# A retention and expert kernel: the first expert in plain fp32, zeroed columns in the activations, one program order on every engine

## The chip, the cores and the metric

The kernel runs on one core of a Trainium2 chip. The metric is the device time of one execution in microseconds (us). The core has five engines with queues of their own, each of which works strictly in the order of its instructions: PE (TensorE, the matmuls; "PEld" is its loading of weights), DVE (VectorE), ACT (ScalarE), POOL (GpSimd) and SP (SyncE, which here only issues DMA transfers). POOL issues the indirect transfers, those that scatter rows to addresses held in a table. Engines wait for one another by semaphores.

## What is computed

Two stages follow each other. The first is a retention layer (attention with a decay and no softmax) over 8 batches, 8 heads, 576 positions and head size 64; its output is read as 4608 tokens of 512 numbers. The second is a mixture of experts: 16 experts in 4 groups of 4. Each token goes to one expert, chosen by two argmaxes, and is scaled by the product of the two softmax weights.

```python
scores = scale * np.matmul(q, k.transpose(0, 1, 3, 2))
ret = scores * Dmat[None, :, :, :]            # Dmat = gamma ** (i - j) for i >= j, else 0
x = np.matmul(ret, v)                         # -> (4608, 512)
...
for g in range(G):                            # 4 groups
    ...
    for e in range(Eg):                       # 4 experts in each
        mask_e = e_idx == e
        h = np.maximum(xg[mask_e] @ w1[g, e], 0.0)      # 512 -> 1024
        ye = h @ w2[g, e]                               # 1024 -> 512
        combined = g_w[mask_g][mask_e] * e_w[mask_e]
        out[tok_idx] = combined[:, None] * ye
```

All inputs and the output are fp32, and an expert's weights are 4 MB.

## The kernel before

**Attention.** The 36 token tiles of 128 (`t`) go through a software pipeline, the loop at line 618: `scale(t + 1)` makes the decayed values `vs` (eight small ACT copies a tile; for the last four tiles one POOL operation), `scores(t)` (PE, then the mask on DVE, `sT`), `av(t - 1)`, `state(t)` and `inter(t - 1)` (PE; DVE writes the tile's x transposed, `xT`), and behind them by some tiles `logits`, `gate`, `places` (which expert a token goes to and its place in that expert's list) and `xnat`, which turns x, scales it and scatters its rows with an indirect transfer to the DRAM table `xs`, sorted by expert. Attention's matmuls are plain fp32.

**The order of experts.** The passes `p` = 0 to 15 run over the experts by load: the two fullest are picked early (`pick(0)` and `pick(1)`), the others are ranked by count once all tokens are placed (`rank_experts`, a run of DVE operations). Each pass has a fixed capacity of columns, `CAPS`, from 356 for p = 1 down to 260 for p = 15. Pass 0 takes the first 256 tokens of the fullest expert, and the last pass, p = 16, the rest of that expert's 384. What doesn't fit is left to a loop at the end.

**One expert.** `xload` (SP) fetches the expert's rows of x in 32-row blocks (`xb`), `xturn` transposes them on DVE into `xTf`, `xsplit` splits them in two fp32r parts, high (ACT copy, `xTh`) and low (DVE subtraction, `xTl`). Each weight piece (four for each expert, w1 and w2) is loaded raw (`r`), and `split` makes its high and low parts, `wh` on ACT and `wl` on DVE, two halves each. A product is then three fp32r matmuls: high by high, high by low, low by high. `layer1(p, f)` makes 128 of the 1024 hidden units: 12 matmuls into `ph`, ACT's relu `hh` (high part) and DVE's `hl` (low part). `layer2(p, f)` adds them to the sums `py` in PSUM with another 12 matmuls (p = 0 and 16 lay tokens on the output rows instead, and p = 0 takes 6). Eight values of f make an expert. PE runs `layer1(p, f)` and then `layer2` of the step before, so that the last layer2 of an expert comes behind the first layer1 of the next. There `yturn` (DVE) transposes the four finished sums out of PSUM, and `ystore` scatters them to `out` with POOL's indirect transfers, two blocks of 32 tokens in each of the following steps.

DVE transposes in blocks of 32, so where a capacity is no multiple of 32, the columns of `py` up to the next multiple must hold numbers. `layer2` zeroes them by a memset of each of the four sums at f = 0, ahead of its matmuls:

```python
            if not natural(p) and CS[p] % 32:
                for py in pys[p]:
                    dve.memset(py[:, CS[p] : 32 * nblocks(p)], 0.0)
```

`xpad(p)` is one more indirect POOL transfer: it zeroes the 128 rows behind an expert's tokens in `xs`, ahead of that expert's `xload`. The code issues one in each pass, two passes ahead.

**Queues and their order.** Every engine call goes through the wrapper `Ordered` (line 95), whose one line, 106, is therefore the line of nearly every instruction in the profile; instructions are told apart by their tiles. `pin` (line 91) ties an instruction behind the one that stands before it in its engine's list, by `keep_in_program_order`. Instructions that the wrapper doesn't see, such as the register moves in front of an indirect transfer, are not tied themselves, and a transfer pinned behind such a move is free to go where the move goes. Within these ties a scheduler chooses the order when the kernel is built.

Of the kernel before, what the change touches and what calls it, by code (L numbers as in the profile page):

```python
# [15 lines left out]
P = 128  # L16
# [4 lines left out]
E = G * EG  # L21
# [44 lines left out]
def moe_retention(ctx, tc, qk, kv, wgt, w1, w2, c_f, out):  # L66
# [23 lines left out]

    def pin(inst):
        tc.keep_in_program_order(inst)
        return inst
# [59 lines left out]
    def split_piece(i, part):  # L153
        if i < len(pieces):
            wsp[i, part] = wsplit(*pieces[i], raws[i], part)

# [80 lines left out]
    def xturn(p, part, of):  # L237

        if part == 0:
            xTs[p] = xpair(f"m{p}")  # L240
            xTf[p] = ring(f"xTf_{p}")[:, 0 : NKC * CMAX].rearrange("p (k c) -> p k c", k=NKC)
        nb = nblocks(p)
        b0, b1 = nb * part // of, nb * (part + 1) // of
        dve.transpose(
            xTf[p][:, :, 32 * b0 : 32 * b1].rearrange("p k (b t) -> p b k t", t=32),
            xg[p][:, b0:b1, 0:DQ].rearrange("p b (k f) -> p b k f", f=32),
        )
# [172 lines left out]
    def pick(j):  # L420


        def t_(nm, n=1):
            return sm.tile([P, n], F32, name=f"{nm}{j}", tag=nm)

        eh = eah[j]
        pc = ps_sm.tile([P, E], F32, name=f"pc{j}", tag="sm")
        pe.matmul(pc, ones, ohc, start=True, stop=True)
        k0 = t_("k0", E)
        dve.scalar_tensor_tensor(k0, pc, float(E), eid, ALU.mult, ALU.subtract)  # L430
        if j:
# [9 lines left out]
        picked[j] = f0  # L441
        if j:
            return

        k2 = t_("k2", E)
        dve.tensor_tensor(k2, eh, pc, ALU.mult)
        c0 = t_("c0")
# [12 lines left out]
    with ExitStack() as ac:  # L460
# [58 lines left out]
        def scale(t):  # L519

            T = tiles[t]
            T["vs"] = ap.tile([P, H, D], F32, name=f"vs_{t}", tag="vs", bufs=3)
            if t >= PICK + 6:

                pool.tensor_tensor(
                    T["vs"], T["v"], gk[:, T["c"], :].unsqueeze(2).to_broadcast([P, H, D]), ALU.mult
                )
                return
# [89 lines left out]
        for t in range(NT + 1):  # L618
# [26 lines left out]
            if r == 5:  # L645
                pick(0)
                expert_of(0)
            if r in (5, 6, 7, 9):
                load_piece((5, 6, 7, 9).index(r))
            if r == 7:  # L650
                xload(0)
                split(0)
            if r == 8:
                split(1)
                for i in range(2):
                    xturn(0, i, 2)
            if t == NT:
                for kc in range(NKC):
                    xsplit(0, kc)
                split(2)  # L660
# [6 lines left out]
    def count_experts():  # L667
# [7 lines left out]
        pad(pad1, picked[1], n1, 32 * nblocks(1))  # L675
        xpad(1)

    def rank_experts():
# [18 lines left out]
        with nc.allow_low_precision("integers below 16"):  # L697
            dve.tensor_reduce(order, kk, AX.X, ALU.add)

# [7 lines left out]
        dve.tensor_scalar(mia, kk[:, :, 0:NB], float(BIG), None, ALU.mult)  # L707
        cb, ce = [sm.tile([P, E], F32, name=f"c{x_}", bufs=1) for x_ in "be"]
# [10 lines left out]
    def layer1(p, f):  # L719
        i = p * NPIECE + f // 2  # L720
        C = CS[p]
        wh, wl = wsp[i, 0]
        xh, xl = xTs[p]
# [5 lines left out]
        cs = slice((f % 2) * P, (f % 2) * P + P)  # L729
        n = 0  # L730
# [6 lines left out]
        hh = mp.tile([P, CMAX], F32R, name=f"hh_{p}_{f}", tag="hh", bufs=4)  # L737
# [7 lines left out]
    def layer2(p, f):  # L745
        if f == 0:
# [4 lines left out]
            if not natural(p) and CS[p] % 32:  # L751
                for py in pys[p]:
                    dve.memset(py[:, CS[p] : 32 * nblocks(p)], 0.0)
        C = CS[p]
        wh, wl = wsp[p * NPIECE + f // 2, 1]
        hh, hl = hts.pop((p, f))
        st_, sp_ = f == 0, f == NFC - 1
        if natural(p):
            for i, (r0, n) in enumerate(ttiles(p)):
                py = pys[p][i]  # L760
                for m, (a, b) in enumerate(((hh, wh), (hh, wl), (hl, wh))):
                    pe.matmul(
                        py[:n], a[:, r0 : r0 + n], b[:, f % 2, :], start=st_ and m == 0, stop=sp_ and m == 2
                    )
            return
        for dc in range(NKC):
            py = pys[p][dc]
            ds_ = slice(dc * P, (dc + 1) * P)
            pe.matmul(py[:, :C], wh[:, f % 2, ds_], hh[:, :C], start=st_, stop=False)
# [70 lines left out]
    prev = None  # L840
    for p in range(E):
        for f in range(NFC):
# [17 lines left out]
            split(2 * pc + f % 2 + 3)  # L860
# [14 lines left out]
            if (p, f) == (0, 4):  # L875
                rank_experts()
# [3 lines left out]
            if f == (2 if p > 0 else 5) and p + 2 <= E:  # L880
# [308 lines left out]
```

## Time and profile before

| | us |
|---|---|
| median of three runs | 733.26 |
| lowest and highest | 727.58, 739.38 |
| the profiled execution | 735.81 |
| its span, first to last instruction | 734.0 |
| attention, to the first matmul of p = 0 | 173.7 |
| p = 0, to the first matmul of p = 1 | 31.9 |
| p = 1 to 15, to the first matmul of the last pass | 498.9 |
| the last pass and the end | 29.6 |

The profile is of one execution. Its page gives busy time by engine, groups of instructions and the chain of waits; other views cut the span in stretches, list the instructions in order of time, or sum up who waited for whom. A row such as "PE py <- DVE py: 48.1, 14, 13.8" says that PE's instructions that write `py` waited for a DVE instruction that writes `py`: 48.1 us in all, 14 times, at most 13.8. In a row of a timeline stand start, duration, engine, operation, output and inputs, shapes, how many, and in brackets the idle time ahead of it and what ended it. "PEclk" is the TensorE clock that was granted, as a share of full speed. The releaser "remote" stands for a semaphore whose sender the profile couldn't place in time.

### The profile page before, as it was taken

The numbers are of one execution on the slowest core, as the hardware profiler recorded it, in microseconds if no ns is written. First come the engines' busy times: TensorE is split into PE (matmuls) and PEld (weight loads), VectorE is DVE, ScalarE is ACT, GpSimd is POOL, SyncE is SP. The second block draws the span as 40 slices with busy tenths as digits, with TensorE's granted clock in tenths as the row PEclk, the third lists the DMA queues.
The fourth block names the chain that finished last, engine by engine and source line by source line (L and its number), as shares of the span: only waits on it lengthen the run. The fifth ranks groups of instructions, "written<-read, shape, count | busy, mean of one in ns | idle before, by whom it ended". The sixth has DMA issues, their size and how long they took to land.

```text
span 734.0 us, 15587 instructions
## 1 busy us (share of the span) xinstructions
PE 633.8 (86%) x5707; PEld 589.3 (80%) x5707; DVE 447.8 (61%) x1093; ACT 325.7 (44%) x829; POOL 230.4 (31%) x258
## 2 busy tenths in 40 slices
PE   7999999987847979878979889898998988889891
PEld 6778787766737979878969889898898988889891
DVE  2677777779843639584637384655656638366580
ACT  3877677534432424332515253343434525335360
POOL 0032222342470060835050505224152140422532
PEclk8999999999987999998999899999999999999997
DMA  9998898573887653149555474646567567465200
GB/s 341 408 387 305 297 332 283 206 254 128 268 257 239 195 167 116 36 137 314 152 152 153 148 207 143 200 134 177 168 194 219 157 179 204 136 184 152 92 16 22
DMA packets 63262, 144.22 MB, mean 196 GB/s; under 512 B 9393, under 2 KB 30393, under 8 KB 63184
## 3 DMA queue, kind: packets, MB, share of 16 engines
q1 hardware_dynamic: 52640, 121.00, 52.5%
q0 software_dynamic: 9248, 20.35, 7.6%
q10 hardware_dynamic: 1296, 1.86, 0.7%
q8 instruction: 46, 0.75, 0.4%
q14 instruction: 32, 0.26, 0.1%
HBM read 122.84 MB, written 24.88 MB: 201 GB/s over the span
## 4 chain that ended last, share of the span: by engine, by line
PE 46%; issue 13%; DVE 6%; POOL 5%; ACT 2%; another core or an unknown queue 2%; DMA 1%; POOLq 0%; ACTq 0%
PE py L106 23%; PE ph L106 22%; DVE wl L106 3%; POOL out L106 3%; ACT wh L106 1%; DVE y L106 1%; POOL xs L106 1%; ACT hh L106 1%; PE phn L106 1%; DMA xs<-zero,pads 1%; DVE hl L106 0%; PE pxt L106 0%; POOL ov_big L106 0%; POOL ov_small L106 0%
## 5 line engine op out<-in xcount | busy, mean ns | idle before, releaser
L106 POOL DMA_INDIRECT out<-y,ii x152 | 156.9, 1032 | 335.1 <-DVE y L106 293.3
L106 PE MATMUL py<-hh,wh 128*128 128x356 f32 (+14 forms) x480 | 151.8, 316 | 59.2 <-DVE py L106 48.1
L106 ACT ACTIVATE hh<-ph 128x256 fp32r<-128x256 f32 (+15 forms) x128 | 53.9, 421 | 298.3 <-PE ph L106 208.6
L106 DVE SCALAR_TENSOR_TENSOR hl<-ph,hh 128x256 fp32r<-128x256 f32 (+15 forms) x128 | 59.3, 464 | 198.7 <-ACT hh L106 156.7
L106 DVE TENSOR_TENSOR wl<-r,wh 128x512 fp32r<-128x512 f32 x272 | 176.8, 692 | 5.2 <-ACT wh L106 1.7
L106 PE MATMUL ph<-xTh_m,wh 128*128 128x256 f32 (+15 forms) x512 | 160.1, 313 | 1.8 <-ACT xTh_m L106 1.2
L106 PE MATMUL ph<-xTl_m,wh 128*128 128x256 f32 (+15 forms) x512 | 159.3, 311 | 0.9 <-issue 0.6
L106 PE MATMUL ph<-xTh_m,wl 128*128 128x256 f32 (+15 forms) x512 | 158.5, 310 | 0.4 <-issue 0.4
L106 PE MATMUL py<-hl,wh 128*128 128x356 f32 (+14 forms) x480 | 151.8, 316 | 4.0 <-DVE hl L106 4.0
L106 ACT CAST wh<-r 128x512 fp32r<-128x512 f32 x272 | 153.7, 617 | 0.0
L106 PE MATMUL py<-hh,wl 128*128 128x356 f32 (+14 forms) x480 | 149.9, 312 | 0.0
L106 PEld LDWEIGHTS py<-hh,wh 128*128 128x128 f32 x480 | 94.7, 197 | 64.5 <-issue 34.4
L106 PEld LDWEIGHTS ph<-xTh_m,wh 128*128 128x128 f32 x512 | 102.8, 201 | 2.1 <-ACT xTh_m L106 1.4
L106 PEld LDWEIGHTS ph<-xTl_m,wh 128*128 128x128 f32 x512 | 102.2, 200 | 2.3 <-issue 1.7
L106 PEld LDWEIGHTS ph<-xTh_m,wl 128*128 128x128 f32 x512 | 101.6, 198 | 1.2 <-issue 1.1
L106 PEld LDWEIGHTS py<-hl,wh 128*128 128x128 f32 x480 | 95.3, 199 | 6.8 <-DVE hl L106 6.8
L106 PEld LDWEIGHTS py<-hh,wl 128*128 128x128 f32 x480 | 95.0, 198 | 0.0
L106 POOL DMA_INDIRECT xs<-xt,sl x36 | 37.0, 1028 | 141.2 <-ACT vs L106 41.4
L106 ACT ACTIVATE vs<-b,cf 128x64 f32<-128x64 f32 x256 | 64.4, 336 | 4.8 <-DMA b<-in_kv 4.8
L106 DVE TENSOR_TENSOR sT<-pss,masks 128x512 f32<-128x512 f32 x72 | 46.2, 683 | 28.0 <-PE pss L106 26.5
L106 PEld LDWEIGHTS pss<-a 64*128 64x128 f32 x576 | 39.4, 192 | 18.4 <-DVE sT L106 8.8
L106 PE MATMUL pss<-a 64*128 64x128 f32 x576 | 48.5, 293 | 5.2 <-DVE sT L106 2.9
(160 smaller groups left out, 604.3 us busy)
## 6 DMA issues: line engine op xcount, KB each, us to landing
r<-in_w SPq DMA_DIRECT2D x138, 512.0 KB
a<-in_qk SPq DMA_DIRECT2D x35, 512.0 KB
b<-in_kv SPq DMA_DIRECT2D x35, 512.0 KB
xb<-xs SPq DMA_DIRECT2D x24, 148.5 KB
xb<-xs SPq DMA_DIRECT2D x20, 165.0 KB
out<-y,ii POOLq DMA_INDIRECT x152
xb<-xs SPq DMA_DIRECT2D x12, 181.5 KB
gq<-c_f ACTq DMA_DIRECT2D x5, 256.0 KB
```

Source lines behind the costliest of these rows:

```text
L106: i_ = f(*a, **k)
```

## The change

- **First expert whole.** For p = 0 (`whole(p)`) the weights and x aren't split. `layer1` is four plain fp32 matmuls, raw w1 by `xTf`, `layer2` one for each of the two token tiles, and the relu writes fp32; `hl`, `xsplit(0)` and the splits of the first eight half pieces are gone.
- **Zeroed columns.** The memsets of `py` are gone. `layer1` at f = 0 zeroes the columns of `hh` from the capacity to the next multiple of 32, and the first matmul of each sum at f = 0 runs over these columns too.
- **Program order.** `pin` now ties each wrapped instruction to the last wrapped instruction of the same engine, whatever stands between.
- **Ranking in parts.** `rank_experts` is a generator: the order of experts at (0, 4), the tables for unused places at (0, 5), the rest at (0, 6), where the register for p = 2 is loaded too. `xpad(2)` moves from (0, 5) to (0, 7), and `xturn(1)` and `xsplit(1)` one step later.
- **Around the first expert.** `pick(0)` is cut in two: its second half, `close`, runs one tile later. `xload(0)` comes one tile earlier, the two halves of `xturn(0)` stand in two tiles instead of one, and `scale` uses ACT for all tiles.

```diff
     def pin(inst):
-        tc.keep_in_program_order(inst)
+
+        i_ = inst.ins
+        if i_.engine in last:
+            tc.add_manual_dep(
+                i_, last[i_.engine].name,
+                mybir.DependencyInfo(mybir.DependencyClass.NoSync, mybir.DependencyReason.DATA),
+                reason="order of the program",
+            )
+        last[i_.engine] = i_
         return inst
...
-            xTs[p] = xpair(f"m{p}")
+            xTs[p] = None if whole(p) else xpair(f"m{p}")
...
-            if t >= PICK + 6:
-
-                pool.tensor_tensor(
-                    T["vs"], T["v"], gk[:, T["c"], :].unsqueeze(2).to_broadcast([P, H, D]), ALU.mult
-                )
-                return
...
+            if r == 6:
+                close()
             if r in (5, 6, 7, 9):
                 load_piece((5, 6, 7, 9).index(r))
-            if r == 7:
+            if r == 6:
                 xload(0)
-                split(0)
-            if r == 8:
-                split(1)
-                for i in range(2):
-                    xturn(0, i, 2)
+            if r in (8, 9):
+                xturn(0, r - 8, 2)
             if t == NT:
-                for kc in range(NKC):
-                    xsplit(0, kc)
-                split(2)
                 ids(0)
...
+        hh = mp.tile([P, CMAX], F32R, name=f"hh_{p}_{f}", tag="hh", bufs=4)
+        if whole(p):
+            for kc in range(NKC):
+                pe.matmul(
+                    ph[:, :C], raws[i][0][:, kc, cs], xTf[p][:, kc, :C], start=kc == 0, stop=kc == NKC - 1
+                )
+            act.activation(hh[:, :C].bitcast(F32), ph[:, :C], AF.Relu)
+            hts[p, f] = (hh.bitcast(F32), None)
+            return
...
+        C32 = 32 * nblocks(p)
+        if f == 0 and C32 > C:
+
+            dve.memset(hh[:, C:C32].bitcast(F32), 0.0)
...
-            if not natural(p) and CS[p] % 32:
-                for py in pys[p]:
-                    dve.memset(py[:, CS[p] : 32 * nblocks(p)], 0.0)
...
-                for m, (a, b) in enumerate(((hh, wh), (hh, wl), (hl, wh))):
+                ab = ((hh, wh),) if whole(p) else ((hh, wh), (hh, wl), (hl, wh))
+                for m, (a, b) in enumerate(ab):
...
+        C0 = 32 * nblocks(p) if st_ else C
...
-            pe.matmul(py[:, :C], wh[:, f % 2, ds_], hh[:, :C], start=st_, stop=False)
+            pe.matmul(py[:, :C0], wh[:, f % 2, ds_], hh[:, :C0], start=st_, stop=False)
...
-            split(2 * pc + f % 2 + 3)
+            if 2 * pc + f % 2 + 3 >= 2 * NPIECE:
+                split(2 * pc + f % 2 + 3)
...
-            if (p, f) == (0, 4):
-                rank_experts()
+            if (p, f) in ((0, 4), (0, 5)):
+                next(ranks, None)
+            if (p, f) == (0, 6):
+                next(ranks, None)
+                expert_of(2)
...
-            if f == (2 if p > 0 else 5) and p + 2 <= E:
+            if f == (2 if p > 0 else 7) and p + 2 <= E:
                 xpad(p + 2)
...
-            if f == NFC - 3:
+            if f == (NFC - 3 if p else NFC - 2):
                 for i in range(3):
                     xturn(p + 1, i, 3)
-            if f == NFC - 2:
+            if f == (NFC - 2 if p else NFC - 1):
                 for kc in range(NKC):
                     xsplit(p + 1, kc)
```

More of the change, by code (lines that the diff above doesn't have):

```diff
@@ L89, in moe_retention @@
     ones = cp.tile([P, P], BF16, name="ones")
+    last = {}
     def pin(inst):
-        tc.keep_in_program_order(inst)
+        i_ = inst.ins
[6 more added lines that the diff above has]
+        last[i_.engine] = i_
         return inst
@@ L155, in split_piece, with whole @@
             wsp[i, part] = wsplit(*pieces[i], raws[i], part)
+    def whole(p):
+        return p == 0
     def split(k):
@@ L440, in pick, with close @@
         dve.tensor_copy(eai[j], f0)
-        picked[j] = f0
-        if j:
-            return
-        k2 = t_("k2", E)
+        picked[j] = f0, pc
+    def close():
+        f0, pc = picked[0]
+        eh = eah[0]
+        k2 = sm.tile([P, E], F32, name="k2")
         dve.tensor_tensor(k2, eh, pc, ALU.mult)
-        c0 = t_("c0")
+        c0 = sm.tile([P, 1], F32, name="c0")
         dve.tensor_reduce(c0, k2, AX.X, ALU.add)
@@ L522, in scale @@
             T["vs"] = ap.tile([P, H, D], F32, name=f"vs_{t}", tag="vs", bufs=3)
-            if t >= PICK + 6:
-                pool.tensor_tensor(
-                    T["vs"], T["v"], gk[:, T["c"], :].unsqueeze(2).to_broadcast([P, H, D]), ALU.mult
-                )
-                return
             for h in range(H):
@@ L674, in count_experts @@
         dve.tensor_reduce(n1, c1, AX.X, ALU.add)
-        pad(pad1, picked[1], n1, 32 * nblocks(1))
+        pad(pad1, picked[1][0], n1, 32 * nblocks(1))
         xpad(1)
@@ L698, in rank_experts @@
             dve.tensor_reduce(order, kk, AX.X, ALU.add)
+        yield
         cr = sm.tile([P, E], F32, name="cr")
@@ L707, in rank_experts @@
         dve.tensor_scalar(mia, kk[:, :, 0:NB], float(BIG), None, ALU.mult)
+        yield
         cb, ce = [sm.tile([P, E], F32, name=f"c{x_}", bufs=1) for x_ in "be"]
@@ L721, in layer1 @@
         C = CS[p]
-        wh, wl = wsp[i, 0]
-        xh, xl = xTs[p]
         if p == 0:
@@ L729, in layer1 @@
         cs = slice((f % 2) * P, (f % 2) * P + P)
+        hh = mp.tile([P, CMAX], F32R, name=f"hh_{p}_{f}", tag="hh", bufs=4)
[7 more added lines that the diff above has]
+            return
+        wh, wl = wsp[i, 0]
+        xh, xl = xTs[p]
         n = 0
@@ L736, in layer1 @@
                 n += 1
-        hh = mp.tile([P, CMAX], F32R, name=f"hh_{p}_{f}", tag="hh", bufs=4)
+        C32 = 32 * nblocks(p)
+        if f == 0 and C32 > C:
+            dve.memset(hh[:, C:C32].bitcast(F32), 0.0)
         hl = mp.tile([P, CMAX], F32R, name=f"hl_{p}_{f}", tag="hl", bufs=4)
@@ L750, in layer2 @@
             ]
-            if not natural(p) and CS[p] % 32:
-                for py in pys[p]:
-                    dve.memset(py[:, CS[p] : 32 * nblocks(p)], 0.0)
         C = CS[p]
-        wh, wl = wsp[p * NPIECE + f // 2, 1]
+        wh, wl = (raws[f // 2][1], None) if whole(p) else wsp[p * NPIECE + f // 2, 1]
         hh, hl = hts.pop((p, f))
@@ L760, in layer2 @@
                 py = pys[p][i]
-                for m, (a, b) in enumerate(((hh, wh), (hh, wl), (hl, wh))):
+                ab = ((hh, wh),) if whole(p) else ((hh, wh), (hh, wl), (hl, wh))
+                for m, (a, b) in enumerate(ab):
                     pe.matmul(
-                        py[:n], a[:, r0 : r0 + n], b[:, f % 2, :], start=st_ and m == 0, stop=sp_ and m == 2
+                        py[:n], a[:, r0 : r0 + n], b[:, f % 2, :],
+                        start=st_ and m == 0, stop=sp_ and m == len(ab) - 1,
                     )
             return
+        C0 = 32 * nblocks(p) if st_ else C
         for dc in range(NKC):
@@ L840, in moe_retention @@
     prev = None
+    ranks = rank_experts()
     for p in range(E):
```

## The prediction

> **What bounds the kernel now.** I began with the page, to see which engine could set the end.
>
> ```profile
> span 734.0 us, 15587 instructions
> PE 633.8 (86%) x5707; PEld 589.3 (80%) x5707; DVE 447.8 (61%) x1093; ACT 325.7 (44%) x829; POOL 230.4 (31%) x258
> ```
>
> PE is the busiest, yet 14% of the span has no matmul in it. An average over stages says nothing about where. So the second view was busy time by stretch, cut at the first layer-1 matmul of each expert (columns: stretch, its length, then busy time of PE, PEld, DVE, ACT, POOL, the granted clock, the DMA share, GB/s). First all fifteen experts of 24 matmul groups each (p = 1 to 15) in one row, then four of them (p = 1, 2, 9 and 10).
>
> ```profile
> 205.53:704.42 498.89, 433.80 (x2875) 424.11 (x2874) 291.03 (x621) 195.39 (x426) 164.34 (x157) 0.94 0.57 168
> ```
>
> ```profile
> 205.53:252.94 47.41, 33.35 (x187) 32.50 (x186) 20.85 (x44) 16.24 (x34) 12.00 (x12) 0.86 0.76 235
> 252.94:287.78 34.84, 30.84 (x194) 30.05 (x193) 19.98 (x44) 13.35 (x28) 12.80 (x13) 1.00 0.54 162
> ...
> 497.29:529.64 32.35, 28.13 (x195) 27.48 (x193) 18.46 (x41) 12.73 (x29) 10.24 (x10) 0.95 0.59 169
> 529.64:555.81 26.17, 26.17 (x195) 25.73 (x193) 16.38 (x33) 11.96 (x28) 10.65 (x10) 1.00 0.67 193
> ```
>
> The row at 529.64 is the find of this profile. It is p = 10, whose capacity is 288. It takes 26.17 us, has PE busy for all of it and the clock at 1.00. Its neighbour in the row above (292 columns, 1.4% more work) takes 32.35 us. 288 is the only capacity from 356 down to 260 that is a multiple of 32, so it is the one expert for which layer2 issues no memset of its sums. The third view, the waits, says the same thing:
>
> ```profile
> PE py L106 <- DVE py L106: 48.1, 14, 13.8
> PE py L106 <- ACT hh L106: 11.0, 8, 3.6
> PE py L106 <- DVE hl L106: 4.0, 2, 2.2
> DVE ov_bt L106 <- POOL ov_small L106: 5.8, 1, 5.8
> ```
>
> PE waited 14 times, once for each of the other fourteen, for "DVE py", which is that memset: 48.1 us, one time 13.8, so the other thirteen mean 34.3 / 13 = 2.6 us. The timeline at the start of p = 5 (PE, then DVE) shows how:
>
> ```profile
> 368.76 0.31 PE L106 MATMUL ph<-xTh_m,wl 128*128 128x314 f32 x1
> 371.65 0.39 PE L106 MATMUL py<-hh,wh 128*128 128x314 f32 x1 [2.58 <-DVE py L106]
> ```
>
> ```profile
> 367.83 1.84 DVE L106 STREAM_TRANSPOSE y<-py 128x352 f32<-128x352 f32 x4
> 369.63 0.48 DVE L106 SCALAR_TENSOR_TENSOR hl<-ph,hh 128x314 fp32r<-128x314 f32 x1
> 370.14 1.29 DVE L106 TENSOR_TENSOR wl<-r,wh 128x512 fp32r<-128x512 f32 x2
> 371.44 0.09 DVE L106 MEMSET py<- 128x6 f32 x4
> ```
>
> PE could go on at 369.07. The sums had been read out (transposes) by 369.67, the first of the four by about 368.3. But the memset stands in the DVE queue behind the rest of hl and a pair of weight splits, and PE gets its first sum only at 371.65. After such waits the clock falls, here before and after 414.20, p = 6:
>
> ```profile
> 407.40:414.20 6.80, 6.13 (x24) 6.16 (x25) 0.55 (x5) 0.00 (x0) 5.12 (x6) 0.50 0.42 129
> 414.20:417.60 3.40, 3.40 (x25) 3.40 (x25) 1.78 (x3) 1.46 (x3) 2.79 (x3) 1.00 0.17 58
> ```
>
> 24 matmuls in 6.8 us at 0.50 against 25 in 3.4 us at 1.00. At a mean of 0.94 over 498.89 us, the half clock costs 6%, some 30 us. That has a rule beside it. The Trainium skill ("TensorE: Matmul & The Clock Gate", section "Why this matters for your kernels") asks for no PE-idle gaps over about 3 us, since an idle window halves the clock. By that the 2.6 us waits are too short to do it, and the half clock would stay when they go; that is a rival below.
>
> **The change part by part.**
>
> *Zeroed columns in hh.* Fourteen groups of four memsets leave layer2; one DVE memset (each 0.09 or less) for f = 0 is issued in layer1, ahead of hl, on a ring buffer that PE last read half an expert earlier. Ahead of it in the queue stand only things hl also waits for. The first matmul of each sum is up to 28 columns wider: 4 x 28 x 0.46 ns per column (the 314-column matmuls follow each other by about 0.145 us) is 0.05 us, nothing. What is late next at 369.07? hh and hl of f = 0 were made before these rows, the first sum is free at about 368.3, the others follow each 0.46 us while PE needs three matmuls, 0.44 us, for one: no wait. So I take p = 10 as the model: 26.17 us / 288 = 0.0909 us a column, and the fifteen capacities sum to 4520 columns: 410.7 us for 498.9, a gain of 88.2. The parts agree: 48.1 + 15.0 of waits and 30 of clock are 93. p = 10 had no wait for hh; others did, and these I don't remove: 11.0 us kept, and 1 for the clock after the longest. The 4.0 for hl come in p = 3, where DVE stood behind the overflow tables' POOL operations (the row "ov_bt", 5.8 us), which POOL had put behind ten `out` transfers; in program order two to four stand ahead of each, so these go. Fifteen experts: 410.7 + 12 = 422.7, **-76.2**.
>
> *Program order.* PE, ACT, DVE and SP run in program order already; POOL does not:
>
> ```profile
> 198.37 0.97 POOL L106 DMA_INDIRECT xs<-zero,pads  x1 [4.58 <-DVE el L106]
> ...
> 217.36 0.97 POOL L106 DMA_INDIRECT xs<-zero,pads  x1 [0.30 <-issue]
> ```
>
> All fifteen pad transfers, which the code issues one per expert, run from 198.37 to 218.3 in one burst, ahead of the first expert's `out`. In that burst PE's messages to ACT come late:
>
> ```profile
> 211.26 0.33 PE L106 MATMUL ph<-xTh_m,wl 128*128 128x356 f32 x1
> 225.35 0.64 PE L106 MATMUL py<-hh,wh 128*128 128x356 f32 x1 [13.76 <-DVE py L106]
> ```
>
> ```profile
> 222.82 0.47 ACT L106 ACTIVATE hh<-ph 128x356 fp32r<-128x356 f32 x1 [5.20 <-remote]
> ```
>
> ACT takes at 222.82 a ph that PE finished at 211.6, and DVE, the memset and PE stand behind it. With the pads spread out I expect this 13.8 to go (it is inside the 76.2). Bounds: it stays whole, +14, or goes whole. I take the second, because both things that feed it, burst and memset, leave. Each later expert gets one pad in its queue: 1.0 to 1.3 us on POOL, which is busy 10 of 30 us. Behind it wait only `out` transfers; the xb load of the next expert waits for a pad issued an expert earlier. Price 0, or +1 for each of 14 if the bursts hold PE's messages longer.
>
> *First expert in fp32.* Per f, 12 split matmuls of 256 columns took 1.40 us and 6 of 512 took 1.39 (chain rows):
>
> ```profile
> 180.72 1.40 PE ph L106 x12
> 182.12 1.39 PE py L106 x6
> ```
>
> Plain fp32 stands in the attention: 36 tiles of 8 sT products are 576 records, two to a matmul.
>
> ```profile
> L106 PE MATMUL px<-sT,vs 128*64 128x128 f32 x576 | 41.6, 289 | 4.4 <-DVE xT L106 4.4
> ```
>
> ```profile
> 161.54 1.09 PE L106 MATMUL px<-sT,vs 128*64 128x128 f32 x16
> 159.67 0.85 PE L106 MATMUL plt<-xT,wgp 128*32 128x384 f32 x8
> ```
>
> 16 records, two side by side in the array: 7 steps in 1.09 - 0.289, 0.114 us per 128 columns. So 256 columns cost 2 x 2 x 0.114 = 0.457, four of them 1.83; 512 cost 0.915, two of them 1.83. 3.66 against 2.79 us, +0.87 x 8 = **+7** (the 384-column logits, two records of four side by side, step by about 0.35, 0.117 per 128 columns: +7.7; a tenth less than the first: +4). What it takes off: 16 halves of wh and wl, 8 hl, the xT split, some 11 us of ACT and 16 of DVE.
>
> ```profile
> L106 DVE TENSOR_TENSOR wl<-r,wh 128x512 fp32r<-128x512 f32 x272 | 176.8, 692 | 5.2 <-ACT wh L106 1.7
> ```
>
> ```profile
> 173.66:205.53 31.87, 27.69 (x181) 23.43 (x181) 27.11 (x86) 17.03 (x37) 14.53 (x19) 0.95 0.66 223
> ```
>
> DVE was as full as PE here (27.11 and 27.69 of 31.87), and PE waited for its queue:
>
> ```profile
> 198.81 0.50 PE L106 MATMUL py<-wh,hl 128*128 128x512 f32 x1 [2.29 <-DVE mil L106]
> 204.49 0.50 PE L106 MATMUL py<-wh,hl 128*128 128x512 f32 x1 [1.07 <-DVE xTf L106]
> ```
>
> Both wait for hl, which no longer exists: -3.4, and -1.6 for the 5% of clock after the first. The next thing late is x of p = 1: its loads can start only when the last pieces of x are scattered, which moves little, and transpose and split come one f later. I put 1 there (0 to 4). Sum for this stage: +7 - 5 + 1 = **+3**. The ranking in three parts is in these 2.29. The raw weights stay in the ring until PE has read them; piece 7, asked for at f = 5, needs the buffer that layer2 leaves at f = 2: nothing. On SP, the register load for p = 2 moves to f = 6, ahead of piece 8; piece 7 is in front of it: nothing.
>
> *Attention's end.* PE waited here too:
>
> ```profile
> 168.59 1.97 PE L106 MATMUL px<-sT,vs 128*64 128x128 f32 x16 [4.44 <-DVE xT L106]
> 173.66 0.38 PE L106 MATMUL ph<-xTh_m,wh 128*128 128x256 f32 x1 [1.20 <-ACT xTh_m L106]
> ```
>
> DVE was in two weight splits and then waited for xb, which now is asked for a tile earlier, and only half the transposes stand ahead of sT. Of 5.6 us I take 3 (0 to 6, since the transposes still wait for a ring buffer that PE frees). Against it, scale of four tiles moves to ACT, 32 copies instead of four operations:
>
> ```profile
> L106 ACT ACTIVATE vs<-b,cf 128x64 f32<-128x64 f32 x256 | 64.4, 336 | 4.8 <-DMA b<-in_kv 4.8
> 140.00:173.66 33.66, 26.11 (x389) 20.90 (x387) 25.48 (x86) 9.46 (x20) 12.25 (x18) 0.90 0.56 191
> ```
>
> 32 x 0.336 = 10.8 us on an engine busy 9.46 of 33.66: hidden, as the same copies were for 32 tiles before; without that cover up to +5. **-3**.
>
> *Sum.* The profiled execution took 735.81 us, 2.5 above the median of the three runs (733.26; 727.58 to 739.38). 735.8 - 76.2 + 3 - 3 = 659.6; on the median's footing **657**.
>
> **The rivals.**
> *The wait only moves (0.07).* If the memset still ends up ahead of the first sum, for instance by hh waiting for it behind DVE's splits, thirteen waits of 2.6 and their clock (23: the 30 less p = 1's 14% of 47.41) stay: 657 + 34 + 23 = 714. Against it: the queue position read above.
> *The half clock isn't the waits' (0.06).* Then the 23 stay alone: 680. For it: p = 2 has the wait and a clock of 1.00. Against it: of the quoted experts only those with the wait fall below 1.00.
> *The bursts take it back (0.14).* ACT waited 36 us in all for late messages while POOL sent `out` in bursts,
>
> ```profile
> ACT hh L106 <- remote: 36.0, 7, 8.7
> ```
>
> and part of that was hidden behind the memset wait and the half clock. If all of it shows on PE (36 - 11 = 25) and each costs a half-clock window (14 x 1.7): 657 + 49 = 706; half of it, 680.
> *Slower (0.03).* A pad in every burst holds PE's messages as the pads did at 211. Fifteen pads cost 14 us there, 1 each; it decides only when each of 14 costs over 5.5 us, more than all of 76.2. At 6.5: 748.
> *Cleaner than I say (0.04).* All like p = 10, attention's 6: 640.
>
> **How the numbers follow.** The forecast (0.66) spans 642 to 672: the kept 12 gone or doubled, first expert 0 to +7, attention 0 to -6. The range goes from 642 to 692, which takes in the half clock rival and over half of the bursts: 0.66 + 0.06 + 0.08, 0.80. A change under 2% (14.7 us, about what three runs spread by) can't be told from none. Faster by over 2%, below 718.6: 0.66 + 0.06 + 0.14 + 0.04 + 0.05 of the first rival is 0.95; within 2% 0.02; slower 0.03.
>
> **What would show it.** The waits of PE for "DVE py" gone; every expert stretch near 0.091 us a column with the clock at 1.00; pads one per expert on POOL; no gap of PE over 3 us after p = 0; the first expert's layers at 1.8 us each. I am wrong if PE's first `py` of an expert still waits over a microsecond, if the clock dips stay without waits, or if waits "ACT hh" on PE grow past 25 us.

## The result and the profile after

The kernel after takes 696.8 us (median of four, 692.0 to 697.3), the kernel before beside it 735.1 (727.6 to 739.4): a ratio of 0.950 with a 95% interval of 0.941 to 0.959. The gain is 38 us where the prediction had 76. The profiled execution has a span of 694.9 us, 1.9 below its own time of 696.8. One execution of the kernel before, beside after_again further down, took 794.0 us at a mean granted clock of 0.73 and is left out of the ratios.

The page of the kernel after, its first lines:

```profile
span 694.9 us, 15369 instructions
...
PE 628.4 (90%) x5659; PEld 576.0 (83%) x5659; DVE 430.6 (62%) x1023; ACT 324.6 (47%) x841; POOL 229.9 (33%) x254
```

Busy time by stretch, with the columns of the prediction: first p = 1 to 15 in one row, then p = 1, 2, 3, 8, 10 and 12.

```profile
204.34:665.72 461.38, 426.40 (x2872) 415.21 (x2873) 287.11 (x576) 195.40 (x425) 173.53 (x161) 0.96 0.54 181
204.34:238.00 33.66, 33.00 (x185) 31.57 (x186) 19.67 (x38) 15.67 (x33) 2.92 (x3) 0.95 0.92 303
238.00:274.82 36.82, 33.37 (x193) 31.83 (x193) 19.82 (x41) 13.24 (x28) 13.66 (x14) 0.91 0.48 156
274.82:313.24 38.42, 31.91 (x194) 31.09 (x193) 28.61 (x53) 12.34 (x27) 22.63 (x16) 0.91 0.20 58
441.64:475.21 33.57, 28.38 (x194) 28.09 (x193) 18.62 (x38) 12.81 (x29) 10.76 (x11) 0.95 0.48 157
508.56:536.22 27.66, 26.70 (x194) 25.79 (x193) 16.29 (x33) 11.94 (x28) 12.06 (x11) 1.00 0.49 160
562.95:588.83 25.88, 25.71 (x195) 24.96 (x193) 17.27 (x36) 12.06 (x28) 11.08 (x10) 1.00 0.56 197
```

p = 1 went from 47.4 to 33.7: the stall of 13.8 us is gone. p = 12 is at 25.88 for 280 columns, 0.092 us a column, close to the model's 0.091. But p = 2, 3 and 8 are 6 to 8 us too long: PE stands for 3 to 7 us in each and the clock is 0.91 to 0.95. Over the fifteen experts PE is idle for 35 us and the clock costs 4%, some 18; the prediction had kept 12 for both. The waits of the kernel after say what PE stands for:

```profile
ACT hh L116 <- remote: 56.2, 10, 9.9
PE ph L116 <- issue: 10.4, 21, 1.1
PE py L116 <- ACT hh L116: 9.9, 4, 5.2
DVE ov_bt L116 <- POOL ov_small L116: 9.2, 1, 9.2
PE py L116 <- issue: 7.4, 9, 3.1
PE py L116 <- DVE hl L116: 6.5, 3, 5.5
```

The row "PE py <- DVE py" is gone, with 48.1 us. In its place stand waits for hh behind ACT's "remote", which grew from 36.0 to 56.2 us, matmuls that wait for nothing shown ("issue"), and one wait behind the overflow tables that had been 5.8 and is 9.2. The timeline of POOL and of ACT at p = 8 of the kernel after shows the first kind:

```profile
449.18 0.98 POOL L116 DMA_INDIRECT out<-y,ii  x1 [19.26 <-DVE wl L116]
...
462.01 0.97 POOL L116 DMA_INDIRECT out<-y,ii  x1 [0.30 <-issue]
```

```profile
453.50 0.42 ACT L116 ACTIVATE hh<-ph 128x298 fp32r<-128x298 f32 x1 [1.87 <-PE ph L116]
...
464.87 0.42 ACT L116 ACTIVATE hh<-ph 128x298 fp32r<-128x298 f32 x1 [9.91 <-remote]
```

POOL issues eleven transfers in a row, ten `out` and a pad, one each 1.28 us. ACT hears of a ph that PE finished at 456.8 only at 464.9, 1.9 us after the last of them. PE has run ahead as far as it can and waits 5.2 us. The trace also records when a semaphore is raised. The three matmuls that raise the one for ACT here end at 456.8, 458.3 and 460.2, and the next three raises stand at 464.84, 464.96 and 465.09: the message is late, and not ACT. The prediction had this as its rival "the bursts take it back".

### The profile page after: what moved, and what is told of

It reads as the page before. It is cut to its first block, busy times and chain, and to the rows that moved or that the text cites. A ratio compares the mean times of both kernels' runs of the same rounds, so it can differ in the third digit from the quotient of the medians.

```text
span 694.9 us, 15369 instructions
## 1 busy us (share of the span) xinstructions
PE 628.4 (90%) x5659; PEld 576.0 (83%) x5659; DVE 430.6 (62%) x1023; ACT 324.6 (47%) x841; POOL 229.9 (33%) x254
## 4 chain that ended last, share of the span: by engine, by line
PE 72%; DVE 10%; issue 4%; DMA 4%; POOL 3%; another core or an unknown queue 3%; ACT 1%; SPq 0%; POOLq 0%; ACTq 0%; DVEq 0%
PE py L116 29%; PE ph L116 28%; PE px L116 5%; PE pss L116 4%; PE pxt L116 2%; POOL out L116 2%; DMA b<-in_kv 2%; DVE sT L116 2%; PE plt L116 1%; PE pst L116 1%; DMA xb<-xs 1%; DVE wl L116 1%; POOL ov_small L116 1%; DVE oh L116 1%
## 5 line engine op out<-in xcount | busy, mean ns | idle before, releaser
L116 ACT ACTIVATE hh<-ph 128x256 f32<-128x256 f32 (+15 forms) x128 | 53.7, 420 | 274.4 <-PE ph L116 183.7
L116 DVE TENSOR_TENSOR wl<-r,wh 128x512 fp32r<-128x512 f32 x256 | 166.5, 692 | 7.2 <-ACT wh L116 4.1
L116 PE MATMUL py<-hh,wh 128*128 128x288 f32 (+17 forms) x480 | 150.3, 313 | 15.5 <-ACT hh L116 9.9
L116 DVE SCALAR_TENSOR_TENSOR hl<-ph,hh 128x356 fp32r<-128x356 f32 (+14 forms) x120 | 55.8, 465 | 161.8 <-ACT hh L116 113.8
L116 PE MATMUL ph<-xTh_m,wh 128*128 128x356 f32 (+14 forms) x480 | 147.6, 307 | 7.1 <-issue 6.1
L116 PE MATMUL ph<-xTh_m,wl 128*128 128x356 f32 (+14 forms) x480 | 147.0, 306 | 2.7 <-issue 2.7
L116 PE MATMUL ph<-xTl_m,wh 128*128 128x356 f32 (+14 forms) x480 | 146.9, 306 | 2.2 <-issue 1.6
L116 PEld LDWEIGHTS ph<-xTh_m,wh 128*128 128x128 f32 x480 | 92.4, 193 | 7.6 <-issue 5.5
L116 PEld LDWEIGHTS ph<-xTl_m,wh 128*128 128x128 f32 x480 | 92.3, 192 | 5.6 <-issue 4.6
L116 PEld LDWEIGHTS ph<-xTh_m,wl 128*128 128x128 f32 x480 | 92.3, 192 | 4.5 <-issue 4.5
```

The source lines that it names most:

```text
L116: i_ = f(*a, **k)
```

## The experiments

Each ran beside the kernel before, and that gave the first finding: the kernel before takes 690 to 702 us in most of these comparisons and 728 to 742 in the others. The table calls them "on time" and "late", after what ACT's "remote" row shows in each trace. The raises of PE's semaphore bear the two words out: in the fourteen traces on time the next raise comes within 0.1 us of the end of its matmul, every time; in the six late ones it comes over 1 us behind for 9 (no_out_3) to 59 (z_only_3) of some 520 matmuls. Times are medians of four (o_only of ten), those marked * one execution; the last two columns are stretches of the profiled execution.

| label | edit | before beside it | time | p = 1 | p = 2 to 15 |
|---|---|---|---|---|---|
| (the pair of the prediction) | before | late | 735.1 | 47.4 | 451.5 |
| (the pair of the prediction) | after | late, 735.1 | 696.8 | 33.7 | 427.7 |
| before_again | before, unchanged | on time | 694.7* | 36.5 | 419.8 |
| after_again | after, unchanged | on time, 696.3 | 647.3 | 32.1 | 379.7 |
| after_3 | after, unchanged | on time, 696.4 | 646.2 | 32.1 | 379.7 |
| z_only | before + zeroed columns | on time, 696.7 | 653.4 | 32.0 | 380.8 |
| z_only_2 | the same | on time, 696.4 | 651.5 | 31.4 | 380.8 |
| z_only_3 | the same | late, 736.7* | 687.6* | 42.0 | 405.7 |
| o_only | before + program order | on time, 696.7 | 694.3 | 36.2 | 416.1 |
| zo | before + both | on time, 696.7 | 649.4 | 31.4 | 379.6 |
| zo_again | the same | on time, 696.3 | 650.8 | 32.2 | 379.7 |
| no_out | after, no `out` of experts 1 to 14 | on time, 696.7 | 637.4 | 32.5 | 373.0 |
| no_out_2 | the same | on time, 696.4 | 637.4 | 32.5 | 373.0 |
| no_out_3 | the same | late, 736.7* | 642.4* | 36.7 | 373.0 |
| out_twice | after, `out` twice in p = 5, 9, 13 | late, 741.7* | 728.5* | 32.1 | 467.7 |
| paced | after, `out` spaced | on time, 696.3 | 644.7 | 32.1 | 378.2 |
| paced_2 | the same | late, 741.7* | 646.8* | 32.1 | 379.7 |
| ov_dve | after, tables' products on DVE | on time, 694.0 | 638.8 | 32.1 | 370.8 |
| paced_ov | paced + ov_dve | on time, 694.0 | 638.7 | 32.1 | 371.2 |
| paced_ov_2 | the same | on time, 696.4 | 638.3 | 32.1 | 371.3 |

**The two kernels again, unchanged.**

> The kernel after, unchanged, beside the kernel before. In the runs of the last call the kernel before took 697 us where the pair of the prediction had 735, and the kernel before with two parts of the change took 649 with no wait for late messages at all. Theory A1 (how long POOL's bursts hold PE's messages differs from chip to chip, and the change itself does what it was said to do): where the kernel before takes about 697, the kernel after takes 640 to 650, ratio 0.92 to 0.935, without waits of PE for hh; where it takes about 735 it is 697 again, ratio 0.95, with them. Theory F (the fp32 expert or the moved steps, which those two parts leave out, bring the late messages): 685 to 697 and waits for hh beside a 697 of the kernel before.

> The kernel before, unchanged, with a profile. Theory A1: if it takes about 697, the 13.8 us wait at p = 1 and the late hh are missing or small in its trace, and the thirteen waits of about 2.6 us for the memset and the half clock after them stand as they did; p = 10, without a memset, takes 26 us in both. If it takes about 735, its trace is the one shown.

> The kernel after, as the measure for the other three of this call. Where the kernel before takes 735 to 742: 697. Where it takes about 696: 647.

On time the kernel after takes 647.3, ratio 0.931 (0.923 to 0.938), and 646.2, ratio 0.927 (0.921 to 0.933): a gain of 49 to 50. Its stretches, p = 1 to 15 in the first row and p = 3 in the second, and three waits of before_again:

```profile
203.26:615.03 411.77, 404.67 (x2872) 402.52 (x2873) 290.81 (x576) 195.68 (x425) 176.78 (x161) 0.99 0.59 203
265.49:303.91 38.42, 31.99 (x194) 31.17 (x193) 28.59 (x53) 12.35 (x27) 22.65 (x16) 0.91 0.23 66
```

```profile
PE py L106 <- DVE py L106: 36.9, 14, 3.3
PE py L106 <- DVE hl L106: 7.8, 5, 2.3
DVE ov_bt L106 <- POOL ov_small L106: 2.2, 1, 2.2
```

No row of ACT waiting for "remote" is left in either trace, though POOL's bursts are the same instructions in the same number. The stall at p = 1 is down from 13.8 to 2.6 in the kernel before as it stands (the 3.3 is another expert's). So the first expectation (A1) holds for the times, and theory F falls: the fp32 expert has no part in the late messages. What A1 says of the cause, that it is the chip, is not so: after_3 and z_only_3 ran on the same chip, the one with messages on time, the other late.

**The parts one by one.** The zeroed columns put into the kernel before, without the new order:

```diff
-                for py in pys[p]:
-                    dve.memset(py[:, CS[p] : 32 * nblocks(p)], 0.0)
...
+            dve.memset(hh[:, C:C32].bitcast(F32), 0.0)
...
-            pe.matmul(py[:, :C], wh[:, f % 2, ds_], hh[:, :C], start=st_, stop=False)
+            pe.matmul(py[:, :C0], wh[:, f % 2, ds_], hh[:, :C0], start=st_, stop=False)
```

and the new `pin` put into it without the zeroed columns:

```diff
     def pin(inst):
-        tc.keep_in_program_order(inst)
+        i_ = inst.ins
+        if i_.engine in last:
+            tc.add_manual_dep(
...
+        last[i_.engine] = i_
         return inst
```

> The kernel before with one part of the change: the zeroed columns in hh in place of the memsets of the sums. Program order, first expert and ranking stay as they were, so the fifteen pad transfers still run in one burst on POOL at about 198 to 218. Theory A (POOL's bursts hold PE's messages to ACT, wherever they run): PE's waits for 'DVE py' go, but the 13.8 us at p = 1 stay in the main as a wait for hh, because that burst stands; the bursts of out are one transfer shorter than in the kernel after, and the later experts lose no more than there. 735 - 34 (thirteen waits of 2.6) - some 5 to 15 of clock = 686 to 700. Theory B (the burst at 198 and the memset together made the 13.8): it goes here too, about 675 to 685. Theory C (the memsets did nothing to the end): 735.

> The kernel before with the other part alone: the unbroken program order, so each pad transfer stands ahead of the out transfers of one expert, and the overflow tables' POOL operations stand between them. The memsets stay. Theory A (POOL's bursts hold PE's messages): the wait of 13.8 us at p = 1 goes down to about 2.6; the other waits for 'DVE py' stay; the bursts of out are one transfer longer, which costs 0 to 1 us each: 735 - 11 - 5 (clock at p = 1) + 0 to 14 = 719 to 733. Theory D (a pad in each burst is what took the gain back in the kernel after): the later experts get longer by 2 us each and the time is 735 or more.

> The kernel before with both parts, the zeroed columns and the unbroken order; the first expert still by split products and the ranking in one piece. The difference to the kernel after is then what the plain fp32 expert and the moved steps at the end of the attention are worth. By the stretches of the two traces p = 0 took 1.7 us longer in the kernel after and the attention ended 2.9 us earlier: 697 + 1 = 698, within 2% of the kernel after. If the fp32 expert frees DVE and ACT for more than that, 702 or more; if it costs its 7 us and gives nothing back, 690.

> The kernel before with the zeroed columns and the unbroken order alone, on the same chip as the kernel after. Where the messages are on time: 649, which against the kernel after gives the price of the plain fp32 expert and the moved steps (after 640 to 650: by the stretches of the traces 0 to -5). Where they are late: within 1% of the kernel after, if the late messages have nothing to do with the first expert.

> The zeroed columns alone, with the order of before. Where the kernel before takes 735 to 742: the burst of fifteen pads at about 198 to 218 stays, the other bursts have one transfer fewer. If a pad in each burst costs much (1 us or more in each of ten), 685 to 692, less than the kernel after; if the burst at 198 still costs its 13.8 us without the memset, 705 to 715, more than the kernel after; both together about 697. Where it takes about 696: 653 again.

On time the zeroed columns alone give 653.4, ratio 0.937 (0.931 to 0.944): 43 of the 49 us. The order alone gives 694.3, ratio 0.994 (0.990 to 0.999), some 2 us; both 649.4; the rest of the change takes some 3 more, out of the attention's end (p = 0 begins at 174.4 in zo_again and at 169.7 in after_again, which ran together). z_only came out far below the 686 to 700 of theory A, since that expected late messages and there were none. For the same reason o_only decides nothing between its theories A and D, and the 698 expected of zo, worked out from the late pair, tests nothing on time. The stretch p = 2 to 15 of z_only, with that of before_again under it (two kernels):

```profile
240.77:621.54 380.77, 373.47 (x2691) 372.78 (x2689) 270.88 (x540) 180.12 (x392) 159.84 (x145) 0.99 0.65 195
```

```profile
243.15:662.96 419.81, 382.17 (x2690) 378.55 (x2689) 274.76 (x579) 180.06 (x392) 152.85 (x145) 0.98 0.57 173
```

39 us less: PE idle for 7.3 in place of 37.6, and 9 less of matmuls at half clock.

**Where messages are late: what the bursts do.** Three edits of the kernel after. no_out leaves out the `out` transfers. out_twice repeats those of experts 4, 8 and 12 to a scratch tensor. paced lets each wait for an index column that DVE copies at two places of each step f, one transfer at each place, in place of two a step without a wait.

```diff
-                for b in range(2 * (f - 1), 2 * f):
-                    ystore(p - 1, b)
+                pass
```

```diff
                 for b in range(2 * (f - 1), 2 * f):
                     ystore(p - 1, b)
+                    if p - 1 in (4, 8, 12):
+                        ystore(p - 1, b, scr, "scr")
```

```diff
+            ip = gp.tile([P, 1], I32, name=f"ip_{p}_{b}", tag="ip", bufs=16)
+            dve.tensor_copy(ip, iis[p][:, b : b + 1])
+            paced[p, b] = ip
+            ystore(p, b)
...
             layer1(p, f)
+            if p > 1 and f > 0:
+                ypace(p - 1, 2 * f - 2)
...
                 split(2 * pc + f % 2 + 3)
+            if p > 1 and f > 0:
+                ypace(p - 1, 2 * f - 1)
```

> The kernel after without the indirect transfers that write the rows of experts 1 to 14 to the output (the pads, the loads of x and of the weights and every instruction of the other engines stay); most of the output is not written. Theory A (the bursts of out hold PE's messages): the waits of PE for hh and the waits of 0.7 us with 'issue' go, the clock stays at 1.00, and p = 1 to 15 take 411 to 417 us in place of 461: a span of 645 to 651. Theory E (the loads of x with small packets, or the traffic of the weights, hold them, and the bursts only run at the same time): the gaps stay, 688 to 697.

> The kernel after without the out transfers of experts 1 to 14 (most of the output is not written). Where the kernel before takes 735 to 742, theory A (the bursts of out are all of it): 637 to 640, the same as on the chips where messages are on time, and no late message after the pads of p = 0; theory E (traffic of the loads has a share): 650 or more with late messages left. Where it takes about 696: 637 again.

> The kernel after without the out transfers of experts 1 to 14 (most of the output is not written), once more. Where the kernel before takes 735 to 742: 637 to 640 if the bursts of out are all of the loss, 650 or more if the traffic of the loads has a share. Where it takes about 696: 637.

> The kernel after with every out transfer of experts 4, 8 and 12 issued a second time to a scratch tensor, so that the bursts in p = 5, 9 and 13 have 20 to 22 transfers in a row in place of 10 or 11. Where the kernel before takes about 697 (messages on time): theory A (the length of a burst alone makes PE's messages late) expects late hh of 3 to 8 us in these three stretches, + 10 to 25 us; theory A1 (there the chip carries both, and length alone does nothing) expects none, and 645 to 650. Where it takes about 735: the late messages of p = 5, 9 and 13 get twice as late, 697 + 15 to 30.

> The kernel after, with each out transfer of experts 1 to 14 waiting for an index column of its own that DVE copies at two places of each step f (behind hl and behind the weight splits), so that one or two transfers run in each step in place of ten to thirteen in a row. Same work, 150 small copies more on DVE. Theory A (the length of the bursts makes PE's messages late): on a chip where the kernel after has waits for hh, they go and p = 1 to 15 take 415 to 425, 655 to 660 in all; on one where it has none, no change (within 3 us). Theory G (each transfer holds a message for its own time, however they are spaced): the waits turn into ten small ones for each expert, 690 or more.

> The kernel with paced out transfers again, in case the chip is one on which the kernel before takes about 735: theory A 655 to 660, theory G 690 or more. Where the kernel before takes about 697 it is 645 as before.

The kernels no_out and paced told nothing of the bursts where messages were on time: paced is at 644.7, within the 3 us that were forecast, and no_out at 637.4, whose 10 us less than the kernel after lie at p = 3 (31.8 for 38.4) and behind p = 15; its own forecast was for late messages only. Where they were late, all three settle it. Twice the transfers, p = 5 of out_twice, and ACT in its p = 9:

```profile
341.43:388.01 46.58, 32.04 (x194) 30.35 (x193) 19.84 (x41) 13.30 (x29) 23.25 (x23) 0.82 0.45 139
```

```profile
522.91 0.41 ACT L116 ACTIVATE hh<-ph 128x292 fp32r<-128x292 f32 x1 [21.09 <-remote]
```

With 21 transfers in a row ACT waited 21.1 us for one message, and p = 5 took 46.6 us where the kernel after, late, took 32.8; p = 9 and 13 grew by 13.0 and 12.9. These were 11, 10 and 9 transfers more, so each cost 1.25 to 1.43 us, where POOL starts one every 1.28. The whole kernel, at 728.5, is just above the 712 to 727 that were expected. No transfers, then the same transfers spaced, first no_out_3 at p = 1 and from p = 2 on, then paced_2 from p = 1 on:

```profile
204.74:241.41 36.67, 33.38 (x184) 31.53 (x185) 20.09 (x38) 15.57 (x33) 15.78 (x15) 0.95 0.86 284
241.41:614.44 373.03, 371.38 (x2690) 370.57 (x2689) 273.68 (x540) 180.10 (x392) 8.87 (x5) 1.00 0.55 173
```

```profile
204.05:615.79 411.74, 405.82 (x2872) 402.35 (x2873) 294.48 (x717) 195.57 (x425) 180.40 (x161) 1.00 0.59 202
```

Without the transfers p = 2 to 15 takes 373.03 us late and 373.01 on time: they are all of the loss there, and the loads have no share. (At p = 1 no_out_3 has 15 operations on POOL: with no `out` between them, the pads run in a row there, and p = 1 takes 36.7 for 32.5 on time. That is most of why the whole, 642.4, falls between the two forecasts, 637 to 640 and 650 or more.) With all of them, only spaced, p = 1 to 15 takes 411.7 late, the same as the kernel after on time and 1.5 more than paced on time. The whole kernel is at 646.8 beside 741.7, better than theory A's 655 to 660. Theory G, that each transfer holds a message however they are spaced, falls. POOL in p = 9 of paced_2 shows how little spacing does it:

```profile
447.75 1.21 POOL L116 DMA_INDIRECT out<-y,ip  x1 [8.77 <-DVE ip L116]
449.26 0.97 POOL L116 DMA_INDIRECT out<-y,ip  x1 [0.30 <-issue]
450.93 1.25 POOL L116 DMA_INDIRECT out<-y,ip  x1 [0.69 <-DVE ip L116]
...
458.99 0.97 POOL L116 DMA_INDIRECT out<-y,ip  x1 [0.30 <-issue]
462.43 1.25 POOL L116 DMA_INDIRECT out<-y,ip  x1 [2.47 <-DVE ip L116]
```

There are still seven in a row after 450.93, but a pause stands before and behind them. Of ACT's waits for "remote" one is left, of 3.5 us, and PE waits for no hh. The messages themselves still come late: from p = 1 on 32 raises stand over 1 us behind their matmul, one by 6.2 us (46 and 8.1 us in the kernel after, late). Spacing keeps the lateness within what PE can run ahead; it doesn't remove it.

**What a pad in each burst costs.**

> The zeroed columns alone, with the order of before, once more. Where the kernel before takes 735 to 742: 685 to 692 if a pad in each burst is dear, 705 to 715 if the burst of pads at 198 still costs its 13.8 us without the memset, about 697 if both or neither. Where it takes about 696: 653.

The last open step was the pads, which the order moves from one burst at 198 to 218 into the bursts of `out`. z_only_3 has them in the old place and every later burst one transfer shorter. Its p = 1, and p = 2 to 15; then p = 2 to 15 of the kernel after, both late:

```profile
208.43:250.44 42.01, 34.35 (x187) 33.33 (x186) 19.98 (x39) 15.54 (x32) 11.21 (x12) 0.86 0.86 265
250.44:656.17 405.73, 386.73 (x2690) 380.04 (x2689) 267.78 (x540) 179.64 (x392) 159.07 (x145) 0.97 0.58 178
```

```profile
238.00:665.72 427.72, 393.40 (x2689) 383.65 (x2689) 267.44 (x540) 179.74 (x392) 170.61 (x158) 0.96 0.51 171
```

One transfer fewer in each of thirteen bursts (p = 15 has no pad): 405.7 for 427.7, though on time the same two kernels are at 380.8 and 379.7. That is a price of 22.0 + 1.1 = 23 us for the pads, 1.8 a burst. It is a mean over one trace of each kernel and falls unevenly: from p = 2 to 14 the experts differ by -1.4 to +5.4 us, and p = 15 by -0.1. Against it the old burst still costs its stall without any memset, 42.0 for 33.7 at p = 1. The expectation had put 685 to 692 for dear pads alone and about 697 for both; both came, and the time is 687.6. So with late messages the new order lost 23 and won 8, and the zeroed columns alone, at 687.6, were 9 us faster than the whole change (one execution against a median of four, whose lowest is 692.0).

**The overflow tables.** In the kernel after DVE waits for a product on POOL. POOL at p = 3, then DVE:

```profile
281.21 0.98 POOL L116 DMA_INDIRECT out<-y,ii  x1 [19.39 <-DVE y L116]
...
294.58 0.97 POOL L116 DMA_INDIRECT out<-y,ii  x1 [0.30 <-issue]
295.56 1.86 POOL L116 TENSOR_TENSOR ov_big<-ov_big 128x784 f32<-128x784 f32 x1
297.50 1.83 POOL L116 TENSOR_TENSOR ov_small<-ov_big,ov_exc 128x784 f32<-128x784 f32 x1
```

```profile
299.37 0.97 DVE L116 TENSOR_REDUCE ov_bt<-ov_small 128x49 f32<-128x784 f32 x1 [9.17 <-POOL ov_small L116]
300.38 0.21 DVE L116 TENSOR_TENSOR ov_pos<-cf,ov_bt 128x49 f32<-128x49 f32 x1
300.50 0.49 DVE L116 SCALAR_TENSOR_TENSOR hl<-ph,hh 128x330 fp32r<-128x330 f32 x1
```

The program issues two `out` a step, but POOL can begin only when y is there, 6.4 us into the expert; then it works off eight of them and a pad in one go, and the tables' products stand behind all nine. hl stands behind the tables on DVE, PE behind hl. The edit puts the products on DVE:

```diff
-                ovt = overflow_tables(*ov, mp, ring, cnt, cf, req, dve, pool)
+                ovt = overflow_tables(*ov, mp, ring, cnt, cf, req, dve, dve)
```

> The kernel after with the five products of the overflow tables on DVE in place of POOL. In its trace at p = 3 DVE waited 9.17 us for a product that stood on POOL behind eight out transfers and a pad, PE 5.5 us for hl behind it, and the clock ran at half for 6.8 us after. Theory H (POOL's queue position is the cause): the wait goes, p = 3 takes 30 to 31 us in place of 38.4, all in all 7 to 8 us less than the kernel after: 639 to 640 where the kernel before takes 697 and 689 where it takes 735. Rival (DVE with 5 us more work in 20 us is the next thing late): PE waits for hl two to four times by 1 to 2 us, 643 to 646.

> Both: the out transfers paced by index columns and the products of the overflow tables on DVE. Where the kernel before takes about 697 and messages are on time, pacing is worth nothing but the few transfers that stood ahead of the tables' products: the same as the other kernel of this call within 3 us. Where it takes about 735 and PE's messages come late in bursts of ten to thirteen transfers, theory A (the length of the bursts matters) expects 30 to 45 us less than the kernel after has there, 650 to 665, theory G (each transfer holds a message however they are spaced) no less than the other kernel.

> Out transfers paced and the overflow tables' products on DVE. Where the kernel before takes 735 to 742: theory A, 639 to 643, messages late by up to 6 us at times but no wait of PE for hh; theory G 680. Where it takes about 696: 639 again.

638.8 us, as theory H had it (639 to 640): p = 3 went from 38.4 to 29.5, and the rival's waits for hl didn't come. All of p = 1 to 15 of ov_dve:

```profile
204.47:607.31 402.84, 402.18 (x2872) 400.84 (x2873) 291.64 (x581) 195.70 (x425) 171.89 (x156) 1.00 0.60 207
```

PE is busy for all but 0.7 us of fifteen experts, at a clock of 1.00: 402.84 / 4520 = 0.0891 us a column. On time pacing adds nothing to that (638.3 and 638.7), as it was forecast; where messages are late paced_ov was not met. It beats both kernels: 638.3 beside 646.2 for the kernel after and 696.4 for the kernel before, ratio to the latter 0.916 (0.910 to 0.921); and paced alone keeps its 646.8 (one execution) where the kernel after falls back to 697.

## Why the prediction was right and wrong

The direction and the main mechanism were right, the size was half: 696.8 for 657, 5 us above the range. The miss is all in p = 1 to 15, 461.4 for 422.7; of the other stages the attention's end moved by 2.9 for 3, and p = 0 by +1.7 for +3. The 2.9 is in part luck: from 140 us to p = 0 PE's idle time fell only by 1.2 (7.55 to 6.35), and 1.7 is PE's busy time, at a mean clock of 0.94 for 0.90, which the sum didn't have. In p = 0 PE's busy time rose by 4.0 (27.69 to 31.73) for the +7, and its idle time fell by 2.3 (4.18 to 1.87) for the -5 + 1.

*Zeroed columns in hh.* Right. The waits for "DVE py" are gone and nothing of the kind took their place; the part alone gives 43 us on time. The model was even too high: 0.0909 us a column was read off a p = 10 of 26.17 us among late messages, and on time the same stretch of the same kernel takes 25.6; 0.0891 is what ov_dve runs over all fifteen, so 402.8 and not 410.7. The rival "the wait only moves" is out.

*The half clock.* Mostly right. With no waits there is none (ov_dve, 1.00), so the rival "the half clock isn't the waits'" is out too. But the 30 us of it in the kernel before were not all the memsets'. On time it has the same waits and a mean clock of 0.98 from p = 2 on, late 0.95; p = 5 and p = 7 of before_again have the same wait of 2.6 us, and only the second a half clock behind it:

```profile
348.90:379.83 30.93, 28.35 (x194) 28.12 (x193) 19.22 (x41) 13.09 (x28) 11.02 (x11) 1.00 0.60 178
410.01:441.11 31.10, 28.52 (x194) 28.30 (x193) 18.98 (x41) 12.98 (x29) 10.18 (x10) 0.95 0.61 176
```

The Trainium skill's limit ("TensorE: Matmul & The Clock Gate", section "Why this matters for your kernels"), no idle gap over about 3 us, is by these rows not sharp: 2.6 us sometimes halves the clock and sometimes doesn't.

*The waits that were kept.* Here the sum failed first. I kept 12 us: the 11.0 of "ACT hh" that PE showed and 1 of clock. But what late messages cost is not that row alone. From p = 2 on the kernel before takes 451.5 us late and 419.8 on time, 32 us; with the memsets gone and the bursts without a pad it is 405.7 against 380.8, 25 us. By the rows of z_only and z_only_3 12 of these are idle time of PE (19.0 for 7.3) and 13 more busy time (386.7 for 373.5, at a clock of 0.97 for 0.99). The sum had put the clock down to the memset, and the "remote" row with its 36.0 us counted only as far as it showed on PE; the rest of it was left to a rival. The sign that I named for that, waits "ACT hh" on PE past 25 us, didn't come: that row went from 11.0 to 9.9.

*Program order.* Half right, and the step that failed most. The stall at p = 1 goes with the burst of pads, as I said (z_only_3 keeps 42.0 there). But "Price 0, or +1 for each of 14" for a pad in each burst was 1.8 in each of thirteen, 23 us: the burst's length sets how late ACT hears from PE, and in bursts past PE's lead a further transfer costs about its own time (1.25 to 1.43 us each in out_twice). The rival "Slower" had this mechanism with 5.5 as its point of turning; its price was a third of that.

*The overflow tables.* Wrong: "in program order two to four stand ahead of each" counted transfers by the step in which the code issues them, and not by when POOL can start on them. Eight and a pad stood ahead. The 4.0 us that were to go became 5.5 and a half-clock window, 8.9 us by ov_dve against after_again at p = 2 to 15.

Summed up: 402.8 for a clean run, 8.9 for the tables, 25 for late messages with the old bursts, 23 for the pads in them, and 1.6 at p = 1 make 461.3; the trace has 461.4. The terms are differences of these same traces, so that they close is no test of them. Against the 422.7 of the prediction that is 23 for the pads in place of 0, 25 kept in place of 12, 8.9 for the tables in place of 0 and 1.6 at p = 1, less 7.9 for a model that was too slow: 38.6 of the 38.7 missed. The rival "the bursts take it back" was the case that came, between its half (680) and its whole (706), and 0.14 was too little for it.

*First expert in fp32.* The chain of waits of the kernel after has its layers at 1.72 and 1.73 us, where I had 1.83 from the attention's small products:

```profile
178.28 1.72 PE py L116 x4
180.00 1.73 PE ph L116 x8
```

That is +5 and not +7 of PE's time. What it gives back can't be told from p = 0 alone, whose length differs by up to 2.4 us between two profiles of one kernel (34.40 in z_only, 32.05 in z_only_2).

## What to carry to other kernels

Count what stands ahead in a queue from the moment at which its engine can start, not from the step of the program that issues it. When a wait is removed, look at the other waits of the same stage as they are then, the ones that were only slack above all. Spread indirect transfers out rather than let them run in a row, and don't add one to a row that is already near PE's lead.

## What the runs showed of the hardware

PE's messages to ACT came late, by up to 21 us (20.8 between a matmul's end and the raise of its semaphore in out_twice), while POOL issued indirect transfers back to back, in some runs and in others not at all, with the same instructions. SP was slowed as well: in the late trace of the kernel after 28 of its register instructions from p = 1 on took over 0.5 us, all beside POOL's transfers, and in after_again none. Some 40 us of the kernel before hang on it (medians of 735 to 742 for 694 to 697). One transfer fewer in bursts of ten to thirteen took half of the loss (48 to 25 us from p = 2 on), twice the transfers in three experts added 40, and pauses of about 0.7 to 2.5 us within and behind the bursts took all but 1.5 us of it. It isn't the chip as such, since one showed both. What it is that differs between the runs stays open.
